# A decode block forward and backward on one core: a regrouped turn between the two passes

## The chip, the cores and the metric

The kernel runs on one core of a Trainium2 chip. The metric is device time in microseconds (us) of one execution, the median of a few runs. The engines are named as in the profile: PE (TensorE; PEld is its weight load), DVE (VectorE), ACT (ScalarE), POOL (GpSimd) and SP (SyncE). In this kernel SP issues nearly all the loads and POOL all the stores; PE, DVE and ACT compute.

## The reference

The reference is a decode step of one token (model width D = 640) and its gradients: adaptive layer norm, attention of 32 heads over a cache of 8192 positions with head width 192, an output projection, then an MLP of width F = 1536 with a second norm inside it. Cut to what matters here:

```
h  = layernorm(x) * (1 + ca) + sa            # sa, ca, ga, sb, cb, gb from silu(c) @ w_mod
q  = h @ wq;  p = softmax(q k^T / sqrt(192));  o = p v;  ao = o @ wo
x  = x + ga * ao
hb = layernorm(x) * (1 + cb) + sb
x1 = hb                                       # the mixer's shift pads a length-1 sequence with zeros
h2 = gelu(layernorm(x1) @ w3) @ w4
out = x + gb * (x1 + h2)
_out, vjp = jax.vjp(f, x, k_cache, v_cache, wq, wo, w3, w4, c, w_mod);  grads = vjp(grad_out)
```

With one token each weight gradient is an outer product: dW4 is 1536x640, the GELU output times the row `dbo` (the incoming gradient times gb). For each head dV is the probability column times the row `do`, and dK is the column dS times the row q; both have the size of the caches, 32 x 8192 x 192. dS needs dP, the sum over the head width of V times `do`, so V is read a second time in the backward pass. `do` comes from `dao` (the gradient at ao) through wo transposed, and `dao` comes through the norms from dn2 = du @ W3 transposed, where du is the gradient at the MLP's hidden layer.

## The kernel before, in words

The cache of one head is handled as two half tiles, t = 0 and 1, of 128 partitions x 32 positions x 192 (1536 KB each). The forward pass runs over heads with a software pipeline (the loop of line 582): step i loads V of head i-1, scales K of head i-1 by the exponentials on ACT and DVE (`fwd_scale`, L394 and L402), and multiplies V and the scaled K on PE (L419, L427, L435). The backward pass goes from head 31 down to 0 (the loop of line 1266): for each head DVE multiplies V by `do` (`bwd_mult`), PE sums it into dP (L1051), DVE and ACT write dV (`bwd_dv`: ACT 20 rows of 32, L1069, and DVE the others, L1036) and DVE writes dK (`bwd_dk`). Weight gradients are jobs put between the heads; `job_dw4` made three blocks of dW4 on ACT per job in steps 17 to 20, and `job_dw3` followed in steps 21 to 25.

Between the passes lies the turn, lines 659 to 1264. It is one chain of small steps:

- W4 and W3 are loaded into three "big" tiles `w_t[0..2]` (`load_wt`, L536 and L539) in the last two forward steps. `dg_some` takes twelve dot products of W4 rows on DVE.
- PE finishes head 31, then the last projection (`last_ao`). In the PE order, the first group of four W3 blocks is transposed between `last_ao(1)` and `last_ao(2)` (`w3T_some`, PE L682 and a copy out of PSUM on ACT or DVE). W3 has 60 blocks; `tr_bank` hands out half a PSUM tile, four blocks, at a time, so the 15 groups alternate over two PSUM tiles of two banks.
- Norm columns, `u_mm` (L747), GELU and its derivative on columns, the rest of the transposes with the `fwd_kvK` of head 31 between them, then dn2 (L812), the second norm's gradient, `dao_bf`, `do` (L934) and its copies `do_pb`.
- The first stores of the kernel's large outputs follow: dV of head 31, first half, is written into `w_t[3]`, the tile that held the transposed W3, and stored in two parts (L1075).

PE, DVE and ACT run in the order in which the code is written (`pin_order`), and SP and POOL issue their DMAs in program order as well: an instruction that waits holds up all behind it on its engine. Buffers come from pools: "big" has five half tiles, used by K tiles, the `w_t` tiles and later by dV and dK; `fv` has three for V, `fpr` two (the forward products, later V), `bv` one, which lies over space that the forward pass frees late. `ring_load` refills V and wo tiles in the backward pass as `bwd_mult` frees them. Loads of V of heads 29 and 30 for the backward pass are issued at the turn: in the code before, V of 29 at line 600 behind W4 and W3, V of 30 in `ring_load` (L330 and L847); V of head 31 stays in its buffers from the forward pass.

Of the kernel before, what the change touches and what calls it, by code (L numbers as in the profile page):

```python
# [20 lines left out]
def kernel(  # L21
# [72 lines left out]
    def bank(tag, bufs=1, name=None, n=512):  # L94
        return psum[0].tile([P, n], FP32, tag=tag, name=name or "ps_" + tag, bufs=bufs)
# [97 lines left out]
    def act_copy(out, in_):  # L193
        nc.scalar.copy(out=out, in_=in_)  # L194
# [130 lines left out]
    def ring_tile(pool):  # L325
        return pool.tile([P, JH, DH], BF16, name="V_sb", tag="prod" if pool is fpr else "V_sb")

    def load_v(pool, h, t):
        tl = ring_tile(pool)
        nc.sync.dma_start(out=tl, in_=V_hd[h][:, t * JH : (t + 1) * JH, :])  # L330
        return tl

    def fwd_load(h, t):
        if 0 <= h < HQ:
            st[h]["V"].append(load_v(fv, h, t))
        if h + 2 < HQ and (h + 2, t) not in K_st:
            K_st[h + 2, t] = load_k(h + 2, t)
# [192 lines left out]
    def alloc_wt(k):  # L530
        w_t.append(flat(big_tile(f"w_t{k}")))
# [50 lines left out]
    for i in range(1, HQ + 1):  # L582
# [7 lines left out]
        if p:  # L590
            fwd_wo(i - 1, st[i - 1])
        if i == HQ - 1:
            alloc_wt(0)
            load_wt(0)
        if i == HQ:
            alloc_wt(1)
            load_wt(1)
            alloc_wt(2)
            load_wt(2)
            V_b[HQ - 3] = [load_v(fpr, HQ - 3, t) for t in range(2)]  # L600
            dg_some(0, 7)
# [65 lines left out]

    tr_n, tr_ps, w3T_next = [0], [None], [0]

    def tr_bank():  # L670
        k = tr_n[0] % 2
        tr_n[0] += 1
        if k == 0:
            tr_ps[0] = bank("s", 2, "t_ps", 1024)
        return tr_ps[0][:, 512 * k : 512 * (k + 1)]

    def w3T_some(n, copy=act_copy):
        for g in range(w3T_next[0], w3T_next[0] + n):
            t_ps = tr_bank()
            for k in range(4):  # L680
                f, i = divmod(4 * g + k, NDC)
                nc.tensor.matmul(t_ps[:, k * P : (k + 1) * P], lhsT=w3n(i, f * P, (f + 1) * P), rhs=ident_bf, start=True, stop=True)  # L682
            copy(w3T(4 * g, 4), t_ps)
        w3T_next[0] += n
# [22 lines left out]
    last_ao(1)  # L707
    w3T_some(1)
    last_ao(2)
# [7 lines left out]
    dot(jk, xs, cb1, s3[:, 2:3])  # L717
    w3T_some(1)
    fwd_keep(LH, sl)
    w3T_some(1)  # L720
    m3 = tn[:, 0:3]
# [10 lines left out]
    nc.vector.tensor_scalar(out=t1, in0=t1, scalar1=v1[:, 0:1], scalar2=None, op0=ALU.add)  # L732
    w3T_some(3)
    hb_bf = ccol(NDC, "hb_bf", BF16)
# [49 lines left out]
    stt(du_bf, deriv, -1.0, d_g, ALU.mult, ALU.mult)  # L784
    w3T_some(4)
    for q in range(2):
        fwd_kvK(LH, q, sl, True)
        w3T_some(1, (act_copy, dve_copy)[q])
    hcb = ccol(NDC, "hcb")
# [7 lines left out]
    mul(nh, n1_c, h1)  # L797
    for q in range(2, 4):
        fwd_kvK(LH, q, sl, True)
        w3T_some(1, (act_copy, dve_copy)[q - 2])  # L800
    w3T_some(1)
    cs = ccol(6, "cs")
# [4 lines left out]
    dot(jk, dbo_c, cb1, cs[:, 4:5])  # L807
    dot(jk, dbo_c, cbn, cs[:, 5:6])
    dn2_ps = bank("b", name="dn2_ps")
    for f in range(NFC):  # L810
        for i in range(NDC):
            nc.tensor.matmul(dn2_ps[:, i : i + 1], lhsT=w3T(f * NDC + i), rhs=du_bf[:, f : f + 1], start=(f == 0 and i == 0), stop=(f == NFC - 1), skip_group_check=True)  # L812
    nc.tensor.matmul(tn[:, 16:22], lhsT=negd_mat, rhs=cs, start=True, stop=True)
    kb_sb = const.tile([P, 2 * DH], FP32, name="kb_sb")
    fek_cm.__exit__(None, None, None)
# [8 lines left out]
    V_b[HS[0]] = st[HS[0]]["V"]  # L824
    held = {("v", HS[2], 0), ("v", HS[2], 1)}
    wo_src = {(PS[k], cc): st[2 * PS[k] + 1]["wo"][:, cc, :] for k in range(2) for cc in range(3)}
# [9 lines left out]
    def ring_load():  # L836
        while ring_n[0] < len(ring) and (ring_n[0] < NR - 2 or ring_key(ring_n[0] - NR) in freed):
            kind, k, t = ring[ring_n[0]]
            pool = (fv, bv, fpr, fpr, fv, fv)[ring_n[0] % NR]
            ring_n[0] += 1  # L840
            if (kind, k, t) in held:
                continue
            if kind == "v":
                V_b.setdefault(k, []).append(load_v(pool, k, t))
                if k == HS[1]:
                    tl = big_tile("V_sb")
                    nc.sync.dma_start(out=tl, in_=V_hd[k][:, JH:J, :])  # L847
                    V_b[k].append(tl)
            else:
                lo, n = PS[BATCHES[k][-1]], len(BATCHES[k])  # L850
                tl = flat(ring_tile(pool))[:, 0 : 3 * n * D].rearrange("p (c r) -> p c r", r=D)
                nc.sync.dma_start(out=tl, in_=wo_v[:, 3 * lo : 3 * (lo + n), :])
                for hp in range(lo, lo + n):
                    for cc in range(3):
                        wo_src[hp, cc] = tl[:, 3 * (hp - lo) + cc, :]
# [28 lines left out]
    def woT_some(n):  # L884
        for j in range(woT_next[0], woT_next[0] + n):
            t_ps = tr_bank()
            for cc in range(3):
                nc.tensor.matmul(t_ps[:, cc * P : (cc + 1) * P], lhsT=sl["wo"][:, cc, j * P : (j + 1) * P], rhs=ident_bf, start=True, stop=True)
            act_copy(woT2[:, j, :], t_ps[:, 0 : 3 * P])
        woT_next[0] += n  # L890

    woT_some(2)
    bwd_pf_act(HS[0])
    bwd_pf_act(HS[1])
    bwd_pf_dve(HS[0])
    bwd_pf_dve(HS[1])
    g_f = ccol(NFC, "g_f")
    mul(g_f, u, sg)
    g_bf = ccol(NFC, "g_bf", BF16)
    dve_copy(g_bf, g_f)  # L900
    s4 = ccol(4, "s4")
# [5 lines left out]
    nc.tensor.matmul(m4, lhsT=negd_mat, rhs=s4, start=True, stop=True)  # L907
    woT_some(3)
    c6 = ccol(6, "c6")
    dve_copy(c6, tn[:, 16:22])  # L910
    td = ccol(NDC, "td")
    zd = ccol(NDC, "zd")
# [11 lines left out]
    m0d = ccol(1, "m0d")  # L924
    dve_copy(m0d, m4[:, 0:1])
    psum_cm.__exit__(None, None, None)
    psum[0] = ctx.enter_context(tc.tile_pool(name="psum_b", bufs=1, space=bass.MemoryType.PSUM, reuse_waits="tile"))
# [3 lines left out]
    do_pb[PS[0]] = bsm.tile([P, 2 * DH], BF16, name="do_pb", tag="do_pb")  # L931
    for c0 in (DH, 0):
        for j in range(NDC):
            nc.tensor.matmul(do_ps[:, c0 : c0 + DH], lhsT=dao_bf[:, j : j + 1].to_broadcast([P, P]), rhs=woT2[:, j, c0 : c0 + DH], start=(j == 0), stop=(j == NDC - 1))  # L934
        act_copy(do_pb[PS[0]][:, c0 : c0 + DH], do_ps[:, c0 : c0 + DH])
    for cc in range(3):
        nc.tensor.matmul(do_ps[:, 400 + cc : 401 + cc], lhsT=do_pb[PS[0]][0:1, cc * P : (cc + 1) * P], rhs=ident_bf[0:1, 0:1], start=True, stop=True)
# [11 lines left out]
    def mid_mm():  # L949
# [4 lines left out]
        mid_ps["kbc"] = kbc_ps  # L954

    def h2_mm():
        for r in range(NDC):
            for f in range(NFC):
                nc.tensor.matmul(h2_ps[:, r : r + 1], lhsT=w4n(f, r * P, (r + 1) * P), rhs=g_bf[:, f : f + 1], start=(f == 0), stop=(f == NFC - 1))

# [162 lines left out]

    def job_dw4(k):
        o = bso.tile([P, 3, D], BF16, name="dw4", tag="so")
        for cc in range(3):
            tsc(o[:, cc, :], dbo_bc, g_f[:, 3 * k + cc : 3 * k + cc + 1], 0)
        st2.dma_start(out=out_7[3 * k * P : 3 * (k + 1) * P, :].rearrange("(c p) r -> p c r", p=P), in_=o)

    def job_dw3(i):  # L1130
# [70 lines left out]
    for k in range(HH):  # L1201
        J1[1 + k].append(lambda hp=PS[k]: job_dwo(hp))
    for k in range(NFC // 3):
        J1[1 + HH + k].append(lambda k=k: job_dw4(k))
    for k in range(NDC):
        J1[1 + HH + NFC // 3 + k].append(lambda i=k: job_dw3(i))

# [42 lines left out]

    h2_mm()
    bwd_dv(HS[0], 0, 0, 2, w_t[3].rearrange("p (j d) -> p j d", d=DH))
    bwd_dv(HS[0], 1)
    dve_copy(do_bf[:, 3 * PS[0] : 3 * PS[0] + 3], do_ps[:, 400:403])
    bwd_dv(HS[1], 0, 8)
    c_first = fin_c(PS[0], 1)
    bcast_dao()
    q_pb[PS[0]] = pair_bc(bsm, q_bf, PS[0], "q_pb")
    act_copy(kb_sb, kb_ps[:, 0 : 2 * DH])
    mid_mm()  # L1260
    bwd_mult(HS[0], 0)
    ring_load()
    bwd_dv(HS[1], 1)
    bwd_mult(HS[0], 1)
    AHEAD = 2 * NPH
    for i in range(HQ):
# [29 lines left out]
        if i in cps:  # L1296
            fin_c_copy(*cps.pop(i))
        if i == 1:
            mid_cols()
            job_mid()  # L1300
            dve_copy(dmod_bf[:, 2 * NDC : 6 * NDC], dmod_c[:, 2 * NDC : 6 * NDC])
# [44 lines left out]
```

## Time and profile before

| | |
|---|---|
| median of 3 runs | 1400.14 us (1400.01 to 1400.24) |
| the profiled execution | 1400.24 us; its span in the trace 1398.4 us |
| PE, DVE, ACT busy | 849.0, 1081.3, 962.2 us |
| moved by DMA | 570.81 MB: 343.08 MB read, 225.91 MB written |
| mean DMA rate over the span | 407 GB/s |
| chain that ended last | DMA 46%, PE 20%, DVE 18%, issue 7%, ACT 6% |

The page cuts the span into 40 slices of 35 us. Digits give the busy share of each engine in tenths, and a row gives the mean share of the 16 DMA engines and what they moved. An answer by windows gives the same for any stretch: busy time and instruction count of PE, PEld, DVE, ACT and POOL, then the granted TensorE clock (PEclk), the DMA share and GB/s. A timeline line gives start and duration, the operation, what it writes and reads, a count where like ones are merged, and in brackets the idle time before it and who ended it. The chain of waits is followed back from the last instruction; it gives start, length and what held the work up. A DMA answer gives the size of a transfer and the time from its issue to its landing.

### The profile page before, as it was taken

The numbers are of one execution on the slowest core, as the hardware profiler recorded it, in microseconds if no ns is written. First come the engines' busy times: TensorE is split into PE (matmuls) and PEld (weight loads), VectorE is DVE, ScalarE is ACT, GpSimd is POOL, SyncE is SP. The second block draws the span as 40 slices with busy tenths as digits, with TensorE's granted clock in tenths as the row PEclk, the third lists the DMA queues.
The fourth block names the chain that finished last, engine by engine and source line by source line (L and its number), as shares of the span: only waits on it lengthen the run. The fifth ranks groups of instructions, "written<-read, shape, count | busy, mean of one in ns | idle before, by whom it ended". The sixth has DMA issues, their size and how long they took to land.

```text
span 1398.4 us, 28097 instructions
## 1 busy us (share of the span) xinstructions
PE 849.0 (61%) x11512; PEld 667.9 (48%) x11512; DVE 1081.3 (77%) x1317; ACT 962.2 (69%) x2622; POOL 111.7 (8%) x203
## 2 busy tenths in 40 slices
PE   3699999999999998546637552334332344324331
PEld 3577777777777776435536441223222232213220
DVE  3678888888888887689988984876677669679794
ACT  1488887787877786683885696467666767558680
POOL 0000000000000000011110111111111111111011
PEclk9799999999999999565656566666676666766665
DMA  9999999999999999588999999999999999999997
GB/s 393 417 420 419 418 419 421 419 421 419 420 409 418 409 406 376 235 345 342 425 428 424 426 429 428 427 429 426 427 426 425 425 422 422 423 413 428 427 429 295
DMA packets 73183, 570.81 MB, mean 408 GB/s; under 512 B 6878, under 2 KB 19934, under 8 KB 32606
## 3 DMA queue, kind: packets, MB, share of 16 engines
q1 hardware_dynamic: 48736, 343.10, 59.5%
q0 software_dynamic: 24288, 225.92, 38.3%
q8 instruction: 90, 1.47, 0.4%
q14 instruction: 39, 0.32, 0.1%
q10 hardware_dynamic: 30, 0.00, 0.0%
HBM read 343.08 MB, written 225.91 MB: 407 GB/s over the span
## 4 chain that ended last, share of the span: by engine, by line
DMA 46%; PE 20%; DVE 18%; issue 7%; ACT 6%; SPq 2%; POOL 0%; another core or an unknown queue 0%; POOLq 0%; DVEq 0%; ACTq 0%
DMA V_sb<-in_A_v_cache_dram 15%; DMA out_dram<-dV 12%; PE ps_a L419 7%; DMA out_dram<-dK 6%; DVE dK L1036 5%; DVE V_sb L131 5%; PE ps_b L427 4%; DMA wq<-in_A_wq_dram 4%; PE S_ps L361 3%; ACT dV L1069 3%; DMA K_sb<-in_A_k_cache_dram 2%; DMA out_dram<-wq_o 2%; DVE dV L1036 2%; DMA out_dram<-dw 2%; PE kb_ps L435 2%
## 5 line engine op out<-in xcount | busy, mean ns | idle before, releaser
L1069 ACT ACTIVATE dV<-do_pb,PF 128x192 bf16<-128x192 bf16 x1248 | 435.5, 440 | 77.6 <-DMA out_dram<-dK 50.8
L1051 PE MATMUL dP_ps<-V_sb,ident_bf 128*128 128x256 bf16 x1536 | 230.0, 325 | 247.0 <-DVE V_sb L131 246.9
L394 ACT ACTIVATE EK<-K_sb,E_f 128x192 bf16<-128x192 bf16 x1024 | 363.6, 441 | 9.4 <-PE kb_ps L299 3.2
L1051 PEld LDWEIGHTS <-ident_bf 128*128 128x128 bf16 x1536 | 178.2, 117 | 298.5 <-issue 176.4
L1036 DVE TENSOR_TENSOR dK<-dS,q_pb 128x6144 bf16<-128x6144 bf16 (+1 forms) x67 | 212.9, 3211 | 39.1 <-DMA out_dram<-dK 35.3
L131 DVE TENSOR_TENSOR prod<-K_sb,q_pb 128x6144 bf16<-128x6144 bf16 x64 | 214.6, 3353 | 35.4 <-DMA K_sb<-in_A_k_cache_dram 34.8
L131 DVE TENSOR_TENSOR V_sb<-V_sb,do_pb 128x6144 bf16<-128x6144 bf16 x64 | 211.9, 3350 | 6.2 <-DMA V_sb<-in_A_v_cache_dram 6.2
L419 PE MATMUL ps_a<-EK,V_sb 128*128 128x193 bf16 x2048 | 199.1, 249 | 23.5 <-DMA V_sb<-in_A_v_cache_dram 22.3
L419 PEld LDWEIGHTS <-V_sb 128*128 128x128 bf16 x2048 | 172.9, 99 | 43.6 <-DMA V_sb<-in_A_v_cache_dram 35.0
L402 DVE TENSOR_TENSOR EK<-K_sb,P2h 128x1536 bf16<-128x1536 bf16 x128 | 121.5, 950 | 0.0
L1036 DVE TENSOR_TENSOR dV<-P2h,do_pb 128x2304 bf16<-128x2304 bf16 (+1 forms) x63 | 84.9, 1374 | 46.4 <-DMA out_dram<-dV 43.8
L427 PE MATMUL ps_b<-EK,V_sb 128*64 128x193 bf16 x2048 | 111.1, 251 | 0.0
L361 PE MATMUL S_ps<-prod,ident_bf 64*64 64x256 bf16 x3072 | 99.8, 277 | 9.3 <-DVE prod L131 8.9
L361 PEld LDWEIGHTS <-ident_bf 64*64 64x64 bf16 x3072 | 83.3, 109 | 24.7 <-issue 24.0
L427 PEld LDWEIGHTS <-V_sb 128*64 128x64 bf16 x2048 | 83.4, 110 | 21.0 <-issue 21.0
L382 ACT ACTIVATE E_f<-sm_ps,negm 128x64 f32<-128x64 f32 x32 | 10.0, 314 | 83.2 <-DVE negm L380 83.2
L435 PE MATMUL kb_ps<-EK,hot_bf 128*32 128x384 bf16 x1024 | 65.9, 335 | 0.0
L1075 POOL DMA_DIRECT2D out_dram<-dV x63 | 33.7, 534 | 399.7 <-ACT dV L1069 248.5
L194 ACT CAST do_pb<-bc_ps 128x384 bf16<-128x384 f32 x15 | 7.0, 470 | 75.9 <-PE bc_ps L190 75.9
L1162 PEld LDWEIGHTS <-ident_bf 128*128 128x128 bf16 x112 | 14.6, 130 | 90.2 <-issue 87.6
L1120 ACT ACTIVATE wq_o<-wq_bc,ha_f 128x1536 bf16<-128x1536 bf16 x12 | 18.5, 1566 | 48.6 <-DMA out_dram<-wq_o 48.6
L1090 POOL DMA_DIRECT2D out_dram<-dK x67 | 37.1, 554 | 183.5 <-DVE dK L1036 146.1
(317 smaller groups left out, 830.1 us busy)
## 6 DMA issues: line engine op xcount, KB each, us to landing
V_sb<-in_A_v_cache_dram SPq DMA_DIRECT2D x126, 1536.0 KB, 16.9
K_sb<-in_A_k_cache_dram SPq DMA_DIRECT2D x64, 1536.0 KB, 18.9
out_dram<-dV POOLq DMA_DIRECT2D x63, 1536.0 KB, 21.4
out_dram<-dK POOLq DMA_DIRECT2D x63, 1536.0 KB, 22.5
wq<-in_A_wq_dram SPq DMA_DIRECT2D x3, 2560.0 KB, 33.8
wo_t<-in_A_wo_dram SPq DMA_DIRECT2D x16, 480.0 KB, 18.1
out_dram<-dwo POOLq DMA_DIRECT2D x16, 480.0 KB, 20.0
wq<-in_A_wq_dram SPq DMA_DIRECT2D x4, 1920.0 KB, 35.9
```

What stands on the lines that cost most here:

```text
L131: nc.vector.tensor_tensor(out=out, in0=a, in1=b, op=ALU.mult)
L361: nc.tensor.matmul(st["S_ps"][c0 : c0 + 64, r, t * JH : (t + 1) * JH, :], lhsT=ident_bf[64 * r : 64 * r + 64, 64 * r : 64 * r + 64], rhs=p ...
L394: nc.scalar.activation(out=EK[:, jj, 0:DH], in_=K_st[h, t][:, r * JQ + jj, :], func=ACT.Copy, scale=st["E_f"][:, j : j + 1])
L402: nc.vector.tensor_tensor(out=EK[:, NA:JQ, 0:DH].rearrange("p j (d r) -> p j d r", r=2), in0=K_st[h, t][:, r * JQ + NA : (r + 1) * JQ, :]. ...
L419: nc.tensor.matmul(st["A_ps"][:, 0 : DH + 1], lhsT=V_sb[:, r * JQ + jj, a0:a1], rhs=EK[:, jj, 0 : DH + 1], start=(q == 0 and jj == 0), sto ...
L427: nc.tensor.matmul(st["B_ps"][g : g + 64, 0 : DH + 1], lhsT=V_sb[:, r * JQ + jj, b0:b1], rhs=EK[:, jj, 0 : DH + 1], start=(q == 0 and jj < ...
L435: nc.tensor.matmul(kb_ps[g : g + 32, 0 : 2 * DH], lhsT=hot_bf[:, HQ - 1 - h : 2 * HQ - 1 - h], rhs=EK[:, jj : jj + 2, 0:DH], start=(h == 0 ...
L1036: nc.vector.tensor_tensor(out=o.rearrange("p j (d r) -> p j d r", r=2), in0=pairs[:, :, None, :].to_broadcast([P, n, NP2, 2]), in1=vec.rea ...
L1051: nc.tensor.matmul(bst[h]["dP_ps"][:, t * JH : (t + 1) * JH, :], lhsT=ident_bf, rhs=V_sb[:, :, k * DS : (k + 1) * DS], start=(k == 0), sto ...
L1069: nc.scalar.activation(out=o[:, jj, :], in_=doh, func=ACT.Copy, scale=bst[h]["PF"][:, j0 + jj : j0 + jj + 1])
L1075: st2.dma_start(out=dV_hd[h][:, j0 + r0 : j0 + r1, :], in_=o[:, r0:r1, :])
L1090: st2.dma_start(out=dK_hd[h][:, j0 : j0 + n, :], in_=o[:, r0 : r0 + n, :])
```

## The change

Four things change, all of them around the turn.

1. `w3T_some(n)` counts blocks instead of groups of four and fills one PSUM tile (up to eight blocks, 1024 columns) before one copy. The 60 blocks go as 4, 8, 8 before `u_mm`, then 8, 8 (this one copied by DVE), 8, 4, 8, 4, the last four with a `fwd_kvK` ahead of each. The columns that DVE computes after `du_bf` stand ahead of these copies. `woT_some` (wo transposed) goes likewise, in groups of two, two and one.
2. V of heads 31 and 30: the forward pass's second half of V of head 30 goes into a big tile; the first half of V of head 31 is loaded one step earlier, ahead of W4's first nine rows; V of 29 (both halves) is loaded ahead of the rest of W4 and the first part of W3, V of 30 (first half) ahead of W3's second part, and its second half behind it. The old loads in `ring_load` go.
3. dW4 is made at the turn: `dw4_some` multiplies `dbo_bc` by a column of the GELU output on DVE, twelve times, into the parts of `w_t[2]` and `w_t[1]` where W3 was, and POOL stores it in three transfers of 6, 3 and 3 blocks. `job_dw4` goes, and `job_dw3` moves to steps 17 to 21.
4. The order at the start of the backward pass: `h2_mm` now stands between the two halves of `do`; the copies of dao and q (`bcast_dao`, `pair_bc`), the probabilities of head 30 (`bwd_pf`) and `bwd_mult(31, 0)` come ahead of dV of head 30, and `mid_mm` moves behind dK of head 31.

```
     def fwd_load(h, t):
-        if 0 <= h < HQ:
-            st[h]["V"].append(load_v(fv, h, t))
+        if 0 <= h < HQ and len(st[h]["V"]) == t:
+            st[h]["V"].append(load_v(big if (h, t) == (HQ - 2, 1) else fv, h, t))
...
         if i == HQ - 1:
+            fwd_load(HQ - 1, 0)
             alloc_wt(0)
             load_wt(0)
         if i == HQ:
+            V_b[HQ - 3] = [load_v(fpr, HQ - 3, t) for t in range(2)]
             alloc_wt(1)
             load_wt(1)
+            V_b[HQ - 2] = [load_v(fv, HQ - 2, 0)]
             alloc_wt(2)
             load_wt(2)
-            V_b[HQ - 3] = [load_v(fpr, HQ - 3, t) for t in range(2)]
+            V_b[HQ - 2].append(load_v(big, HQ - 2, 1))
             dg_some(0, 7)
...
     def w3T_some(n, copy=act_copy):
-        for g in range(w3T_next[0], w3T_next[0] + n):
-            t_ps = tr_bank()
-            for k in range(4):
-                f, i = divmod(4 * g + k, NDC)
-                nc.tensor.matmul(t_ps[:, k * P : (k + 1) * P], lhsT=w3n(i, f * P, (f + 1) * P), rhs=ident_bf, start=True, stop=True)
-            copy(w3T(4 * g, 4), t_ps)
+        b0 = w3T_next[0]
+        t_ps = bank("s", 2, "t_ps", 1024)[:, 0 : n * P]
+        for k in range(n):
+            f, i = divmod(b0 + k, NDC)
+            nc.tensor.matmul(t_ps[:, k * P : (k + 1) * P], lhsT=w3n(i, f * P, (f + 1) * P), rhs=ident_bf, start=True, stop=True)
+        copy(w3T(b0, n), t_ps)
...
     last_ao(0)
     last_ao(1)
-    w3T_some(1)
+    w3T_some(4)
     last_ao(2)
...
+    w3T_some(8)
+    w3T_some(8, dve_copy)
+    for q, n in enumerate((8, 4, 8, 4)):
+        fwd_kvK(LH, q, sl, True)
+        w3T_some(n)
     dn2_ps = bank("b", name="dn2_ps")
...
+    W4_O = (6, 3, 3)
+
+    def dw4_some(n):
+        for f in range(dw4_n[0], dw4_n[0] + n):
+            tl, c0 = (w_t[2], f * D) if f < W4_O[0] else (w_t[1], W4_R * D + (f - W4_O[0]) * D)
+            nc.vector.tensor_scalar(out=tl[:, c0 : c0 + D], in0=dbo_bc, scalar1=g_f[:, f : f + 1], scalar2=None, op0=ALU.mult)
+            if f + 1 in (W4_O[0], W4_O[0] + W4_O[1], NFC):
...
-    woT_some(2)
-    bwd_pf_act(HS[0])
-    bwd_pf_act(HS[1])
-    bwd_pf_dve(HS[0])
-    bwd_pf_dve(HS[1])
-    g_f = ccol(NFC, "g_f")
-    mul(g_f, u, sg)
-    g_bf = ccol(NFC, "g_bf", BF16)
-    dve_copy(g_bf, g_f)
+    bwd_pf_act(HS[0])
+    woT_some(2)
+    dw4_some(2)
     s4 = ccol(4, "s4")
...
     dve_copy(c6, tn[:, 16:22])
+    dw4_some(1)
...
     dve_copy(m0d, m4[:, 0:1])
+    bwd_pf_dve(HS[0])
+    dw4_some(4)
...
+    do_half(DH)
+    for r in range(NDC):
+        for f in range(NFC):
+            nc.tensor.matmul(h2_ps[:, r : r + 1], lhsT=w4n(f, r * P, (r + 1) * P), rhs=g_bf[:, f : f + 1], start=(f == 0), stop=(f == NFC - 1))
+    do_half(0)
...
-    h2_mm()
     bwd_dv(HS[0], 0, 0, 2, w_t[3].rearrange("p (j d) -> p j d", d=DH))
+    dw4_some(5)
     bwd_dv(HS[0], 1)
-    dve_copy(do_bf[:, 3 * PS[0] : 3 * PS[0] + 3], do_ps[:, 400:403])
-    bwd_dv(HS[1], 0, 8)
-    c_first = fin_c(PS[0], 1)
     bcast_dao()
     q_pb[PS[0]] = pair_bc(bsm, q_bf, PS[0], "q_pb")
-    act_copy(kb_sb, kb_ps[:, 0 : 2 * DH])
-    mid_mm()
+    bwd_pf(HS[1])
     bwd_mult(HS[0], 0)
     ring_load()
+    bwd_dv(HS[1], 0, 8)
+    dve_copy(do_bf[:, 3 * PS[0] : 3 * PS[0] + 3], do_ps[:, 400:403])
+    bwd_mult(HS[0], 1)
+    c_first = fin_c(PS[0], 1)
     bwd_dv(HS[1], 1)
-    bwd_mult(HS[0], 1)
+    act_copy(kb_sb, kb_ps[:, 0 : 2 * DH])
```

More of the change, by code (lines that the diff above doesn't have):

```diff
@@ L325, in ring_tile @@
     def ring_tile(pool):
-        return pool.tile([P, JH, DH], BF16, name="V_sb", tag="prod" if pool is fpr else "V_sb")
+        return pool.tile([P, JH, DH], BF16, name="V_sb", tag="prod" if pool is fpr else "big" if pool is big else "V_sb")
     def load_v(pool, h, t):
@@ L666, in w3T @@
         return w_t[2][:, c0 : c0 + n * P]
[L668 to L675, printed above, removed]
-    def w3T_some(n, copy=act_copy):
-        for g in range(w3T_next[0], w3T_next[0] + n):
-            t_ps = tr_bank()
-            for k in range(4):
-                f, i = divmod(4 * g + k, NDC)
-                nc.tensor.matmul(t_ps[:, k * P : (k + 1) * P], lhsT=w3n(i, f * P, (f + 1) * P), rhs=ident_bf, start=True, stop=True)
-            copy(w3T(4 * g, 4), t_ps)
+    w3T_next = [0]
+    def w3T_some(n, copy=act_copy):
+        b0 = w3T_next[0]
[4 more added lines that the diff above has]
+        copy(w3T(b0, n), t_ps)
         w3T_next[0] += n
@@ L717 @@
     dot(jk, xs, cb1, s3[:, 2:3])
-    w3T_some(1)
+    w3T_some(8)
     fwd_keep(LH, sl)
-    w3T_some(1)
     m3 = tn[:, 0:3]
@@ L732 @@
     nc.vector.tensor_scalar(out=t1, in0=t1, scalar1=v1[:, 0:1], scalar2=None, op0=ALU.add)
-    w3T_some(3)
+    w3T_some(8)
     hb_bf = ccol(NDC, "hb_bf", BF16)
@@ L784 @@
     stt(du_bf, deriv, -1.0, d_g, ALU.mult, ALU.mult)
[L785 to L788, printed above, removed]
     hcb = ccol(NDC, "hcb")
@@ L797 @@
     mul(nh, n1_c, h1)
[L798 to L801, printed above, removed]
     cs = ccol(6, "cs")
@@ L808 @@
     dot(jk, dbo_c, cbn, cs[:, 5:6])
+    g_f = ccol(NFC, "g_f")
+    mul(g_f, u, sg)
+    g_bf = ccol(NFC, "g_bf", BF16)
+    dve_copy(g_bf, g_f)
+    w3T_some(8)
+    w3T_some(8, dve_copy)
+    for q, n in enumerate((8, 4, 8, 4)):
+        fwd_kvK(LH, q, sl, True)
+        w3T_some(n)
     dn2_ps = bank("b", name="dn2_ps")
@@ L813 @@
     nc.tensor.matmul(tn[:, 16:22], lhsT=negd_mat, rhs=cs, start=True, stop=True)
+    dw4_n = [0]
+    W4_O = (6, 3, 3)
[4 more added lines that the diff above has]
+            if f + 1 in (W4_O[0], W4_O[0] + W4_O[1], NFC):
+                m = W4_O[0] if f < W4_O[0] else W4_O[1]
+                nc.gpsimd.dma_start(out=out_7[(f + 1 - m) * P : (f + 1) * P, :].rearrange("(c p) r -> p c r", p=P), in_=tl[:, c0 - (m - 1) * D : c0 + D].rearrange("p (c r) -> p c r", r=D))
+        dw4_n[0] += n
     kb_sb = const.tile([P, 2 * DH], FP32, name="kb_sb")
@@ L824 @@
     V_b[HS[0]] = st[HS[0]]["V"]
-    held = {("v", HS[2], 0), ("v", HS[2], 1)}
+    held = {("v", HS[1], 0), ("v", HS[2], 0), ("v", HS[2], 1)}
     wo_src = {(PS[k], cc): st[2 * PS[k] + 1]["wo"][:, cc, :] for k in range(2) for cc in range(3)}
@@ L844, in ring_load @@
                 V_b.setdefault(k, []).append(load_v(pool, k, t))
[L845 to L848, printed above, removed]
             else:
@@ L884, in woT_some @@
     def woT_some(n):
[L885 to L889, printed above, removed]
+        j0 = woT_next[0]
+        t_ps = bank("s", 2, "t_ps", 1024)[:, 0 : 3 * n * P]
+        for k in range(3 * n):
+            j, cc = j0 + k // 3, k % 3
+            nc.tensor.matmul(t_ps[:, k * P : (k + 1) * P], lhsT=sl["wo"][:, cc, j * P : (j + 1) * P], rhs=ident_bf, start=True, stop=True)
+        act_copy(woT2[:, j0 : j0 + n, :].rearrange("p j m -> p (j m)"), t_ps)
         woT_next[0] += n
+    bwd_pf_act(HS[0])
     woT_some(2)
-    bwd_pf_act(HS[0])
-    bwd_pf_act(HS[1])
-    bwd_pf_dve(HS[0])
-    bwd_pf_dve(HS[1])
-    g_f = ccol(NFC, "g_f")
-    mul(g_f, u, sg)
-    g_bf = ccol(NFC, "g_bf", BF16)
-    dve_copy(g_bf, g_f)
+    dw4_some(2)
     s4 = ccol(4, "s4")
@@ L907 @@
     nc.tensor.matmul(m4, lhsT=negd_mat, rhs=s4, start=True, stop=True)
-    woT_some(3)
+    woT_some(2)
+    woT_some(1)
     c6 = ccol(6, "c6")
     dve_copy(c6, tn[:, 16:22])
+    dw4_some(1)
     td = ccol(NDC, "td")
@@ L931, with do_half @@
     do_pb[PS[0]] = bsm.tile([P, 2 * DH], BF16, name="do_pb", tag="do_pb")
-    for c0 in (DH, 0):
+    def do_half(c0):
         for j in range(NDC):
@@ L954, in mid_mm @@
         mid_ps["kbc"] = kbc_ps
[L956 to L959, printed above, removed]
     def mid_cols():
@@ L1122, in tsc @@
             nc.vector.tensor_scalar(out=out, in0=in_, scalar1=col, scalar2=None, op0=ALU.mult)
[L1124 to L1128, printed above, removed]
     def job_dw3(i):
@@ L1202 @@
         J1[1 + k].append(lambda hp=PS[k]: job_dwo(hp))
-    for k in range(NFC // 3):
-        J1[1 + HH + k].append(lambda k=k: job_dw4(k))
     for k in range(NDC):
-        J1[1 + HH + NFC // 3 + k].append(lambda i=k: job_dw3(i))
+        J1[1 + HH + k].append(lambda i=k: job_dw3(i))
     def add_outer(at, name, view, lo, n, col_bf, rows_f, dram, acc, first):
@@ L1297 @@
             fin_c_copy(*cps.pop(i))
+        if i == 0:
+            mid_mm()
         if i == 1:
```

## The prediction

> **What bounds the kernel now.** I read the page's slices first, then windows around the dip in the middle, then the DMA issues there, the chain of waits and the timelines.
>
> ```profile
> DMA  9999999999999999588999999999999999999997
> GB/s 393 417 420 419 418 419 421 419 421 419 420 409 418 409 406 376 235 345 342 425 428 424 426 429 428 427 429 426 427 426 425 425 422 422 423 413 428 427 429 295
> ```
>
> The transfers run full except in slices 15 to 18, the turn. The windows say where:
>
> ```profile
> 558.00:568.00 10.00, 6.82 (x110) 5.13 (x109) 4.24 (x27) 6.38 (x14) 0.00 (x0) 0.54 0.78 327
> 568.00:576.00 8.00, 5.40 (x114) 3.88 (x107) 3.84 (x29) 2.84 (x7) 0.00 (x0) 0.93 0.56 182
> 576.00:600.00 24.00, 14.04 (x133) 10.79 (x131) 20.23 (x34) 20.15 (x57) 2.68 (x5) 0.50 0.48 199
> 640.00:646.00 6.00, 6.00 (x38) 4.59 (x37) 5.96 (x5) 0.00 (x0) 0.54 (x1) 0.65 0.26 64
> 700.00:1380.00 680.00, 275.71 (x1721) 207.26 (x1721) 525.15 (x402) 455.21 (x1182) 95.00 (x168) 0.66 1.01 425
> ```
>
> Idle DMA time is (1 - share) x length: 2.2 + 3.5 + 12.5 + 4.4 = 22.6 us. After 646 the share is 1.0 to the end: no engine's speed matters there, only bytes. So the change is worth what it does to the idle time of the turn. That turn is a chain of small steps, and it starts when W3 has landed:
>
> ```profile
> w_t<-in_B_w_dram SPq DMA_DIRECT2D x1, 1152.0 KB, 14.1
> w_t<-in_B_w_dram SPq DMA_DIRECT2D x1, 768.0 KB, 12.1
> w_t<-in_B_w_dram SPq DMA_DIRECT2D x1, 480.0 KB, 10.7
> ...
> 538.97 3.36 SPq L539 DMA_DIRECT2D w_t<-in_B_w_dram  x1
> 542.38 1.20 SPq L330 DMA_DIRECT2D V_sb<-in_A_v_cache_dram  x1
> ```
>
> W3's second part (`w_t[2]`) is issued at 538.97 and lands at 553.1; V of 29, behind it, is issued at 542.38 and lands at 556.7 (14.3 in its own answer). The chain and the timelines:
>
> ```profile
> 521.02 16.78 DMA w_t<-in_B_w_dram
> ...
> 554.97 0.26 PE t_ps L682 x4
> ...
> 571.11 1.48 PE dn_ps L812 x60
> ...
> 594.96 7.75 PE dP_ps L1051 x48
> ```
>
> ```profile
> 555.05 0.27 PE L704 MATMUL turn_ps<-o_col_bf,wo_t 128*128 128x1 bf16 x5
> 578.89 3.43 DVE L1036 TENSOR_TENSOR w_t<-P2h,do_pb 128x3072 bf16<-128x3072 bf16 x2 [1.36 <-ACT do_pb L194]
> 603.90 3.36 DVE L1036 TENSOR_TENSOR dK<-dS,q_pb 128x6144 bf16<-128x6144 bf16 x1
> ```
>
> PE reaches the first transposes at 554.83, 1.7 us after W3 is there, and does not wait. The last V half, issued at 546.61, has no landing record; one half tile after V of 30's first (545.09 + 19.0 = 564.1) makes 567.8. So before, 14.7 us of V loads cover the chain behind W3.
>
> **Loads.** Transfers land in the order of issue, one V half every 3.6 to 3.8 us (530.3, 533.9, then `w_t[0]` 537.8 by the chain, 541.6 for V of 31, from issue plus time to landing), also where the mean share falls: some DMA engines trail and stay busy, and a transfer has landed when its last part has. Filling the small gaps at 520 to 536 therefore brings no landing forward. What counts is what stands ahead. Ahead of `w_t[0]` there is now one more V half: 537.8 + 3.7 = 541.5. Ahead of `w_t[2]` there are three more (29 twice, 30 once): 553.0 + 3 x 3.65 = 564.0. The last load still ends at 567.7. SP's waits don't undo this: the K tiles whose places the loads take are scaled by 540 (ACT's rows L394, 2.8 us a quarter), well ahead of these landings.
>
> The late `w_t[0]` delays `dg_some` on DVE, behind it the head's sum, PE's matmuls of head 31 and `last_ao(0)`: 3.7 us, to about 558.8. The group of four transposes in front of `last_ao(2)` then needs `w_t[2]`, and PE takes its work in order: `last_ao(2)` moves from 555.05 to 564.1, **+9.1**. The first delay vanishes in the second.
>
> **Transposes.** A copy of 384 columns takes 0.48 us on ACT, of 512 0.58, so of 1024 about 0.98; on DVE 512 take 0.69, 1024 about 1.25. Before, `u_mm` started 0.8 us after its column was ready, held by a transpose waiting for its copy; with two full tiles in flight it doesn't: **-0.8**. From `du_bf` (564.6) to the end of dn2 (572.6) before took 7.9 us. After: two groups of eight and a `fwd_kvK` (1.0, 1.0, 0.8 us at half clock), the DVE copy, which starts only when the moved columns and g_f are done (1.9 us after du) and so ends at +3.2, then groups and `fwd_kvK` 0.5 + 0.8 + 1.0 + 0.8 + 0.5 and dn2's 60 matmuls, 1.64 to 2.2: 8.4 at half clock, 7.2 at full. **+0.1**, ends -0.7 and +0.5.
>
> **From dn2 to dV.** Before, the reductions of dn2 started 2.25 us late, behind `P2h` and g_f, which waited for ACT's PF (DVE idle 1.80 in front of `P2h`); these go, the m4 matmul comes 0.95 us after dn2 instead of 2.97: **-2.0**. dW4's instructions: 128x1536 takes 0.614 us on DVE (L1122), 128x1280 0.546, so 128x640 about 0.38. Two lie in DVE's wait for dn2, one lies in the chain (+0.4), four run while PE and ACT make `do_pb` and overrun it by 0.35. **+0.75**. First dV: 9.1 - 0.8 + 0.1 - 2.0 + 0.75 = +7.1.
>
> **From do_pb to dK.** Before, 578.86 to 603.90: 25.0 us. After, ACT's second `do_pb` copy stands behind `h2_mm` (1.76) and comes 2.6 us after the first; then twenty dV rows (7.0, as in L1069's x20), the copies of dao and q and PF (1.7): 11.3. DVE, done with its own dV by then (it idles some 5 us for PF, where before it had dV of head 30 to do), takes `P2h` 0.25, V 3.35, dV of 30 2.55, V 3.35, sums 0.75, dV 1.35, three wo rows 2.45, their sums 0.9, dP 0.7, dS 0.35: 27.3 in all, **+2.3**. The gain of taking `mid_mm`'s 2.5 us out of PE's way is in it: PE no longer ends last. SP waits longer too: V of 28 is loaded when dP of head 31 is done, 604.7 instead of 600.1, with nothing late by it.
>
> First dK: 7.1 + 2.3 = +9.4. From there DVE does the same work at 21 us a head up to where DMA ran empty (640 to 645), so the point at which transfers become the bound comes 9.4 later.
>
> **dW4's bytes.** 1.97 MB leave that bound phase. Its stores, at 25.9 to 26.5 GB/s on each of 16 engines (425 GB/s in the windows), take 4.7 us; they now run in the gap behind the turn, which has room (12 us idle by my sum ahead of them). **-4.7**. POOL issues three (0.76 each by L1128's row) where it is idle. ACT loses twelve rows of 0.81 us in a phase bound by DMA: nothing; if that cover were gone, up to 9.7 us would be saved there, but share 1.01 excludes that. dW3 four steps earlier: the same bytes, nothing.
>
> **Sum.** +9.4 - 4.7 = +4.7. Counted the other way, by gaps: loads end at 567.7, wo's batch starts behind the last `fwd_kvK` at 580 (12.3 idle, before 4.5), then 2.6 to the first dW4 store, 1.1 and 4.1 between dV stores, before 5.9, 2.1, 4.5 and 0.5: 20.1 against 17.5, and at the second gap 5.8 against 5.0: +3.4. I take +4 between them: span 1402.4, time 1404.2 from the profiled execution's 1400.24, which is the highest of the three runs and 0.1 above the median.
>
> The granted clock enters here: 0.54 in 558 to 568, 0.93 behind it, 0.50 from 576. The Trainium skill, "TensorE: Matmul & The Clock Gate", section "What's actually happening", says that about 3.4 us of idle PE put it back to half clock and as much busy time frees it. By that page the 5 us for which PE would now wait for W3 cost half clock afterwards, and the sum would be +4.7; by a clock that is full up to dn2 it would be about +2.7. The trace's drop to 0.50 in a stretch where PE waits agrees.
>
> **Rivals.**
> - *W3 does not gate.* Its wait vanishes if `w_t[2]` lands by 558.8, so 5 us earlier than I say; for it speaks that the DMA share dips at 520 to 536 and loads are now issued earlier, against it the landings in strict step. Only `w_t[0]`'s 3.7 remains: 4.0 - 5.4 = -1.4, 1398.8.
> - *Nothing is late (other side).* If the trailing engines catch up in the filled gaps, both land as before: 4.0 - 9.1 = -5.1, 1395.1. It decides from a landing of `w_t[2]` before about 557.
> - *The new order costs more.* If DVE's wait for head 30's PF, or dV of 30 standing behind dW4's store in its buffer, also pushes ACT's next forty rows past DVE, some 5 us come on top: 1409.
> - *The head of the backward pass gains.* If DVE's stall is hidden by a DMA that is full there, +2.3 becomes nothing or less: 1401.5.
>
> **Numbers.** Forecast 0.60; W3 not gating 0.10; nothing late 0.12; order costs more 0.10; hidden stall 0.08. The likeliest own range is 1401.5 to 1407; for 8 in 10 I go to 1397.5 and 1409. A run of this kernel tells about 0.2% (2.8 us) from no change: faster 0.13, same 0.23 (not gating, hidden stall, and the forecast's low end), slower 0.64.
>
> **What would show it.** Right: V of 29 issued near 530, `w_t[2]` landing near 564, PE idle some 5 us in front of the third transpose, the first store (dW4) near 587, DVE idle about 5 us ahead of `bwd_mult(31, 0)`, full share from about 655. Wrong: `w_t[2]` landing before 559, or a first dV store before 585.

## The result

The changed kernel takes 1402.36 us (median of 11 runs, 1401.19 to 1403.64) against 1399.49 us before (11 runs): a ratio of 1.0025, 95% interval 1.0015 to 1.0034. It is slower by 2.9 us; the forecast was slower by 4, 1404.2. The profiled execution took 1402.17 us, its span 1400.4 us, 2.0 more than the profiled span before.

The slices of the page in GB/s (the row of DMA digits is the same as before):

```profile
GB/s 393 418 420 418 418 420 419 420 420 420 419 408 420 411 417 381 193 340 337 425 427 424 428 426 428 427 428 427 426 427 425 425 425 418 426 418 423 429 429 303
```

The same hole at the turn, with slice 16 at 193 GB/s where it had 235. The windows of the changed kernel, in the columns explained above:

```profile
562.00:580.00 18.00, 13.56 (x226) 10.44 (x227) 8.88 (x59) 9.53 (x16) 0.00 (x0) 0.62 0.18 64
580.00:602.00 22.00, 9.39 (x115) 7.07 (x113) 16.77 (x33) 18.16 (x51) 5.19 (x7) 0.57 0.78 293
602.00:646.00 44.00, 15.50 (x108) 12.30 (x106) 41.35 (x70) 34.33 (x97) 5.05 (x9) 0.66 0.99 388
646.00:653.00 7.00, 5.71 (x35) 4.28 (x35) 6.97 (x5) 2.13 (x3) 0.39 (x1) 0.62 0.24 99
653.00:1380.00 727.00, 315.77 (x1966) 241.56 (x1963) 578.87 (x479) 481.50 (x1263) 99.06 (x177) 0.66 1.01 424
```

Idle DMA time, (1 - share) x length, is 14.8 + 4.8 + 0.4 + 5.3 = 25.3 us from 562 to 653. The kernel before, over the same stretch, has 9.7 and 8.8 in the first two windows and 5.1 behind them (share 0.90 in both of those), 23.6 in all; the 22.6 of the prediction left out some shorter stretches and does not compare. The first two lines of the kernel before:

```profile
562.00:580.00 18.00, 12.14 (x168) 8.01 (x164) 8.75 (x55) 8.20 (x19) 0.00 (x0) 0.69 0.46 170
580.00:602.00 22.00, 13.21 (x133) 10.78 (x134) 17.67 (x24) 18.39 (x53) 2.82 (x5) 0.55 0.60 242
```

The difference, 1.7 us from shares of two digits, agrees with the loss that the spans show, 2.0: the bytes are the same 570.81 MB and from 653 on the share is full in both. The hole has moved: now most of it lies ahead of 580, between the last load and the first work that the turn hands on.

Why the turn hands on late, from the DMA answers (size and time to landing), SP's timeline, PE's waits and PE's timeline:

```profile
525.01 0.38 SPq L536 DMA_DIRECT2D w_t<-in_B_w_dram  x1
w_t<-in_B_w_dram SPq DMA_DIRECT2D x1, 1440.0 KB, 16.5
...
543.14 0.38 SPq L539 DMA_DIRECT2D w_t<-in_B_w_dram  x1
w_t<-in_B_w_dram SPq DMA_DIRECT2D x1, 1152.0 KB, 20.8
```

```profile
PE t_ps L678 <- DMA w_t<-in_B_w_dram: 4.6, 1, 4.6
...
563.99 0.40 PE L678 MATMUL t_ps<-ident_bf,w_t 128*128 128x128 bf16 x2 [4.61 <-DMA w_t<-in_B_w_dram]
564.17 0.32 PE L700 MATMUL turn_ps<-o_col_bf,wo_t 128*128 128x1 bf16 x5
```

W4's first nine rows land at 541.5 and W3's second part at 563.9, 10.9 us later than before. PE, done with head 31, waits 4.6 us for it, and `last_ao(2)` starts at 564.17 instead of 555.05. On DVE:

```profile
583.90 3.42 DVE L1041 TENSOR_TENSOR w_t<-P2h,do_pb 128x3072 bf16<-128x3072 bf16 x2
...
594.72 0.23 DVE L879 CAST P2h<-PF 128x128 bf16<-128x128 f32 x1 [4.65 <-ACT PF L875]
594.86 3.35 DVE L131 TENSOR_TENSOR V_sb<-V_sb,do_pb 128x6144 bf16<-128x6144 bf16 x1
...
611.41 3.36 DVE L1041 TENSOR_TENSOR dK<-dS,q_pb 128x6144 bf16<-128x6144 bf16 x1
```

The first dV comes 5.0 us later than before (578.89), the first dK 7.5 (603.90), with a wait of 4.65 us for ACT in between. Of these 7.5 us, dW4's stores, taken out of the bound stretch, give back about 5 (e5, below).

### The profile page after: what moved, and what is told of

Same layout as the page of the kernel before. It is cut to its first block, busy times and chain, and to the rows that moved or that the text cites. A ratio compares the mean times of both kernels' runs of the same rounds, so it can differ in the third digit from the quotient of the medians.

```text
span 1400.4 us, 28087 instructions
## 1 busy us (share of the span) xinstructions
PE 851.4 (61%) x11512; PEld 670.5 (48%) x11512; DVE 1084.7 (77%) x1328; ACT 952.1 (68%) x2603; POOL 111.3 (8%) x202
## 2 busy tenths in 40 slices
DMA packets 73168, 570.81 MB, mean 408 GB/s; under 512 B 6863, under 2 KB 19919, under 8 KB 32591
## 5 line engine op out<-in xcount | busy, mean ns | idle before, releaser
L361 PEld LDWEIGHTS <-ident_bf 64*64 64x64 bf16 x3072 | 84.2, 110 | 24.7 <-issue 24.1
```

The source lines that it names most:

```text
L361: nc.tensor.matmul(st["S_ps"][c0 : c0 + 64, r, t * JH : (t + 1) * JH, :], lhsT=ident_bf[64 * r : 64 * r + 64, 64 * r : 64 * r + 64], rhs=p ...
```

## The experiments

The kernel before was timed anew beside each group of runs (medians 1398.18 to 1399.49 us), so the runs are compared best by their ratio to it; the changed kernel stands at 1.0025.

**Loads as before, all else as changed (e1).** The edit, and the moved lines put back:

```
-            V_b[HQ - 3] = [load_v(fpr, HQ - 3, t) for t in range(2)]
             alloc_wt(1)
             load_wt(1)
-            V_b[HQ - 2] = [load_v(fv, HQ - 2, 0)]
             alloc_wt(2)
             load_wt(2)
-            V_b[HQ - 2].append(load_v(big, HQ - 2, 1))
+            V_b[HQ - 3] = [load_v(fpr, HQ - 3, t) for t in range(2)]
```

> The changed kernel with the loads of V of heads 29, 30 and 31 as before the change; the rest as changed. My theory (W3 lands late behind three V halves and holds the turn): W3's second part lands at 553 instead of 564, PE does not wait for it, the first dV store comes 8.9 us earlier and so does the end: some 9 us under the changed kernel, about 1393. Rival (the loads' order is hidden, the new order of the rest costs the time): within 2 us of the changed kernel, 1402.

Measured: 1392.14 us, ratio 0.9953 (0.9939 to 0.9967), 10.2 us under the changed kernel by the medians. PE's timeline of this run has no wait at the transposes:

```profile
554.76 0.39 PE L697 MATMUL turn_ps<-o_col_bf,wo_t 128*128 128x1 bf16 x10
555.01 0.38 PE L675 MATMUL t_ps<-ident_bf,w_t 128*128 128x128 bf16 x4
555.23 0.27 PE L697 MATMUL turn_ps<-o_col_bf,wo_t 128*128 128x1 bf16 x5
```

W3 lands at 553.0, the first dV starts at 574.41 and the first dK at 602.17. The order and places of these loads alone turn the change from a gain of 7 us into a loss of 3.

**The new loads alone, in the kernel before (e2).** The same lines in the other direction.

> The kernel before with the new order and places of the V loads alone. My theory: PE waits about 5 us for W3, which lands at 564, and the whole turn comes 9.1 us later with nothing to make up for it: about 1408. Rival (loads issued earlier fill gaps and the other parts cost the time): 1399.5 or less.

Measured: 1409.08 us, ratio 1.0078 (1.0065 to 1.0090). PE waits 4.1 us for W3, which lands at 564.0; the first dK starts at 613.26, 9.4 later than before. So the loss doesn't need the rest of the change, and in the kernel before nothing makes up for it.

**W4 and W3 ahead of V of 29 and 30, V of 31's first half still ahead of W4 (e3).**

```
+            alloc_wt(1)
+            load_wt(1)
+            alloc_wt(2)
+            load_wt(2)
             V_b[HQ - 3] = [load_v(fpr, HQ - 3, t) for t in range(2)]
-            alloc_wt(1)
-            load_wt(1)
-            V_b[HQ - 2] = [load_v(fv, HQ - 2, 0)]
-            alloc_wt(2)
-            load_wt(2)
-            V_b[HQ - 2].append(load_v(big, HQ - 2, 1))
+            V_b[HQ - 2] = [load_v(fv, HQ - 2, 0)]
+            V_b[HQ - 2].append(load_v(big, HQ - 2, 1))
```

> The changed kernel with V of 29 and 30 loaded behind all of W4 and W3, but V of 31's first half still ahead of W4's first nine rows. My theory: W3 lands at 553 as before, W4's rows still at 541.5, 3.7 us late, so the dot products of W4 and with them PE are 3.7 us late and PE comes to the first transposes at 558.9 without waiting: 5 us under the changed kernel, about 1397.4. Rival (only W3's landing counts): the same time as with all loads as before, about 1393.

Measured: 1397.29 us, ratio 0.9987 (0.9978 to 0.9996). W3 lands at 552.9, W4's rows at 541.7, and PE comes to `last_ao(2)` without a wait for W3. It is late by the dot products: DVE's last scaled keys of head 31 come 3.7 us later than in e1 (549.49 against 545.75), PE's first `last_ao` 4.5 later (559.24 against 554.76):

```profile
559.49 0.38 PE L678 MATMUL t_ps<-ident_bf,w_t 128*128 128x128 bf16 x4
559.71 0.27 PE L700 MATMUL turn_ps<-o_col_bf,wo_t 128*128 128x1 bf16 x5
```

The half tile ahead of W4 costs about 5 us by itself (e3 against e1), and the three ahead of W3 another 5 (the changed kernel against e3): both delays are there, and in the changed kernel the second hides the first.

**Probabilities of head 30 made at the turn (e4).**

```
     bwd_pf_act(HS[0])
+    bwd_pf_act(HS[1])
...
     bwd_pf_dve(HS[0])
+    bwd_pf_dve(HS[1])
...
-    bwd_pf(HS[1])
     bwd_mult(HS[0], 0)
```

> The changed kernel with one step moved: the probabilities of head 30 (PF on ACT, P2h on DVE) are made at the turn beside those of head 31, so that the V product of head 31 does not wait for ACT's twenty dV rows. My theory: DVE's idle time of 4.65 us ahead of it goes, the first dK comes 4.4 us earlier, and so the end: about 1398. Rival (DMA is full there, or PE or ACT takes the wait's place): 1401 to 1402.

Measured: 1397.74 us, ratio 0.9989 (0.9980 to 0.9998), 4.6 us under the changed kernel. DVE goes straight on:

```profile
588.19 1.35 DVE L1043 TENSOR_TENSOR dV<-P2h,do_pb 128x2304 bf16<-128x2304 bf16 x1
589.46 3.35 DVE L131 TENSOR_TENSOR V_sb<-V_sb,do_pb 128x6144 bf16<-128x6144 bf16 x1
...
606.12 3.36 DVE L1043 TENSOR_TENSOR dK<-dS,q_pb 128x6144 bf16<-128x6144 bf16 x1
```

From the first dV to the first dK it takes 22.8 us, against 27.5 in the changed kernel and 25.0 before: the new order is better than the old one once its one wait is gone (e6 below has the old order beside the same probabilities).

**dW4 by the jobs, as before (e5).** `dw4_some` and its calls taken out, `job_dw4` and its place in the list put back.

> The changed kernel with dW4 made by the jobs between heads 15 to 12 as before, on ACT, and not at the turn. My theory: the turn's chain gets some 0.6 us shorter (three or four instructions of 0.38 us), and 1.97 MB of stores go back into the stretch that DMA bounds, 4.7 us: about 4 us over the changed kernel, 1406.5. Rival (these stores are hidden wherever they are): 0.6 us under it, 1401.8.

Measured: 1406.73 us, ratio 1.0063 (1.0051 to 1.0076), 4.4 us over the changed kernel by the medians and 5.3 by the ratios. dW4 at the turn is worth its bytes: the stores fill idle time, and the first dK is at 611.27 without it and 611.41 with it, so that its instructions cost nothing that lasts.

**The start of the backward pass in the old order (e6).** The last block of the diff undone (with `mid_mm` put back ahead of `bwd_mult(31, 0)`), the probabilities of head 30 at the turn.

> The changed kernel with the start of the backward pass in the old order (dV of head 30's first half ahead of the copies of dao and q, the key sums on PE ahead of dP of head 31, probabilities of head 30 made at the turn). My theory: DVE's idle time for these probabilities goes, but PE's 2.5 us of key sums stand ahead of dP again and dW4's five instructions stay on DVE: from do_pb to the first dK 26 to 27 us instead of 27.5, 1 us under the changed kernel, 1401.4. Rival (the order is the whole cost of that stretch): 2.7 us under it or more, 1399.7.

Measured: 1399.72 us, ratio 1.0010 (1.0001 to 1.0019), 2.6 us under the changed kernel. My figure was 1; the rival's 2.7 is what came. From the first dV to the first dK it took 24.7 us (583.95 to 608.61), about as long as before the change (25.0): dP on PE ends last there, DVE waits 3.0 us for it, and dW4's five instructions, 1.6 us, fit into that wait. Against e4, which differs in the order alone, the old order takes 1.9 us longer in this stretch.

**Four blocks to a copy (e7).** Two groups share a tile, as before:

```
     def w3T_some(n, copy=act_copy):
-        t_ps = bank("s", 2, "t_ps", 1024)[:, 0 : n * P]
-        for k in range(n):
+        t_ps = bank("s", 2, "t_ps", 1024)
+        for g in range(n // 4):
+            half = t_ps[:, 512 * g : 512 * g + 512]
...
+            copy(w3T(b0, 4), half)
```

> The changed kernel with each copy of transposed W3 taking four blocks, as before, in the new order of the work around them. My theory: eight blocks a copy are worth little by themselves, 0.5 us of the chain: 1402.9, not to be told from the changed kernel. Rival (they made all of the 2.4 us that the chain gained between the norm's column and dn2): 1404.8.

Measured: 1409.54 us, ratio 1.0079 (1.0065 to 1.0093): 7 us over the changed kernel, three times what even the rival expected. From the end of `u_mm` to the end of dn2 it took 14.6 us instead of 8.7. PE's timeline:

```profile
573.41 1.01 PE L680 MATMUL t_ps<-ident_bf,w_t 128*128 128x128 bf16 x8 [1.37 <-ACT w_t L194]
576.29 0.59 PE L680 MATMUL t_ps<-ident_bf,w_t 128*128 128x128 bf16 x4 [1.87 <-DVE w_t L197]
...
578.85 0.58 PE L680 MATMUL t_ps<-ident_bf,w_t 128*128 128x128 bf16 x4 [0.67 <-ACT w_t L194]
...
582.71 0.59 PE L680 MATMUL t_ps<-ident_bf,w_t 128*128 128x128 bf16 x4 [0.67 <-ACT w_t L194]
```

In this run PE starts a second group of a tile only when the copy of the first has ended, and stops for the DVE copy too. The granted clock differs as well: it was 0.50 from 564 to 608 here, where the changed kernel had its full clock from 576.3 to 583.1. How much of the 7 us that is, no run separates from the waits. In the changed kernel the same stretch has two short waits:

```profile
573.41 1.03 PE L678 MATMUL t_ps<-ident_bf,w_t 128*128 128x128 bf16 x8
575.54 0.59 PE L678 MATMUL t_ps<-ident_bf,w_t 128*128 128x128 bf16 x4 [0.34 <-ACT w_t L194]
576.80 0.61 PE L678 MATMUL t_ps<-ident_bf,w_t 128*128 128x128 bf16 x8 [0.15 <-ACT w_t L194]
```

**Four blocks, each group in a tile of its own (e9),** to tell the shared tile from the number of copies:

```
-        t_ps = bank("s", 2, "t_ps", 1024)
         for g in range(n // 4):
             b0 = w3T_next[0]
-            half = t_ps[:, 512 * g : 512 * g + 512]
+            t_ps = bank("s", 2, "t_ps", 1024)[:, 0 : 4 * P]
```

> The changed kernel with four blocks a copy again, but each group of four takes a PSUM tile of its own (half of it unused), so that PE need not wait for the copy of the other half of the same tile. Theory (in the run with four blocks and two groups to a tile, PE waits at each second group for the copy just started, 1.28 us a group): those waits go, some stay because the two groups copied by DVE hold both tiles until DVE's columns are done; from the end of u_mm to the end of dn2 about 12 us instead of 14.6 (8.7 in the changed kernel): 1405.5. Rival (the number of copies costs, each with its fixed part): 1409, as with four blocks in shared tiles.

Measured: 1405.83 us, ratio 1.0046 (1.0032 to 1.0060). So about half of e7's loss comes with the shared tile. Waits for ACT of 0.94 us and for DVE of 1.05 remain, and dn2 ends 9.0 us after the start of du (573.01 to 582.01), against 12.4 in e7 and 6.5 in the changed kernel. The clock is a rival here too: it was full from 579.8, 3.5 us later than in the changed kernel.

**The transposes alone, in the kernel before (e10).** `w3T_some` and its calls as in the diff, the rest untouched.

> The kernel before with the transposes of the changed one alone (up to eight blocks a copy, the columns ahead of them; wo's transposes as before). My theory: u_mm starts 0.7 us earlier, dn2 ends some 1.8 us sooner behind du, and all behind it moves by that: 2.5 us under the kernel before, about 1396.5. Rival (DVE waits for head 31's probabilities behind ACT's copies of wo anyway): no change.

Measured: 1395.95 us, ratio 0.9975 (0.9965 to 0.9985), 3.3 us under the kernel before. `u_mm` and du start 0.7 sooner, dn2 ends 2.8 sooner (569.80) and dK starts 2.4 sooner (601.50). Here as well the full clock came sooner, at 566.3 instead of 569.1, and is in these 2.8 us.

**Both remedies (e8): the loads as before and the probabilities of head 30 at the turn.**

> The changed kernel with the loads as before and the probabilities of head 30 made at the turn. My theory: both gains add up, 8.9 and 4.4 us, since the one ends ahead of do_pb and the other begins behind it: about 1389, under both kernels. Rival (DMA is full early, so the second gain has no idle time to take): 1393, as with the loads alone.

Measured: 1386.03 us, ratio 0.9913 (0.9900 to 0.9927): 12 us under the kernel before and 16 under the changed one, the fastest of all. The gains add up: 10.2 in e1 and 4.6 in e4 make 14.8. The windows of this run:

```profile
562.00:580.00 18.00, 12.61 (x220) 9.34 (x219) 14.47 (x61) 11.05 (x25) 3.60 (x5) 0.69 0.69 251
632.00:640.00 8.00, 7.29 (x48) 5.50 (x47) 7.97 (x10) 1.27 (x2) 1.49 (x3) 0.72 0.51 170
640.00:1380.00 740.00, 314.40 (x1950) 240.21 (x1950) 576.73 (x474) 481.66 (x1263) 98.52 (x176) 0.66 1.00 422
```

The share in 562 to 580 is 0.69, where the changed kernel has 0.18. What is left idle there is 5.6 us, and 3.9 around 636, where DVE is full.

## Why the prediction was right, step by step

- *Loads land in the order of issue, and filling the dips brings no landing forward.* Right: `w_t[0]` 541.5 (said 541.5), `w_t[2]` 563.9 (564.0), and the loads end as before: the DMA share falls to 0.15 before and 0.10 after in 566 to 568, and to 0.00 behind it. e1, e2 and e3 show that this step carries the sign. The rivals "W3 does not gate" and "nothing is late" fell.
- *`last_ao(2)` +9.1.* Right: 564.17 against 555.05.
- *Transposes.* The term of the sum that was most off. To the start of `u_mm` I had a gain of 0.8; it was 0.4 (+8.7 there), since the 1024-column copy, 1.01 us, stands ahead of the copies that the norm waits for, and the column itself came 9.5 late. From the end of du to the end of dn2 I had 7.9 + 0.1, with ends -0.7 and +0.5: it took 6.3 us (573.36 to 579.66), so -1.6, outside those ends. The step that failed is "the DVE copy, which starts only when the moved columns and g_f are done (1.9 us after du) and so ends at +3.2, then groups": the copy ended at 576.17, 2.8 after du, but PE's next group started at 575.54, 2.2 after du, right behind the ACT copy that had ended at 575.49, and did not wait for DVE. My sum has every group behind the DVE copy wait for it. That is 1.0 of the 1.7 us by which I missed; the other 0.7 lies in the groups and dn2, for which I had taken a value between half and full clock and which ran almost wholly at full clock, granted from 576.3 on.
- *From dn2 to dV, -2.0 + 0.75.* It was 4.2 us against 6.3, so -2.1, 0.8 more of a gain than I said. The reductions came 0.03 us after dn2 (-2.2). dW4's instructions cost about what I said: the one in the chain 0.3, and dV started 0.3 behind `do_pb` for the four. What the sum lacks is the clock at `do`. Its first five matmuls took 0.60 us instead of 0.99, since the clock was full up to 583.1, where before it was 0.50 from 575.9 on. Before and after:

```profile
577.51 0.99 PE L934 MATMUL do_ps<-woT,dao_bf 128*128 128x192 bf16 x5
...
582.66 0.60 PE L938 MATMUL do_ps<-woT,dao_bf 128*128 128x192 bf16 x5 [1.21 <-DVE m0d L197]
```

  First dV: +5.0 instead of +7.1.
- *From do_pb to dK, +2.3.* Right: 27.5 us from dV against 25.0, so +2.5, with the wait for PF (4.65, said some 5). That this wait is the cost is shown by e4.
- *dW4's bytes, -4.7.* Right within the intervals: e5 gives 4.4 to 5.3.
- *Sum.* dK +7.5 (said +9.4), less about 5: 2.0 by the spans, 2.9 by the medians (said 4). The count of gaps gave +3.4 and was nearer than the chain's +4.7; over 562 to 653 the windows give 1.7. By the counts above, about 1 of the 2 us by which dV came sooner than forecast is the clock, whose return at 576.3 the sum did not have; so far the nearness of the figure hangs on luck, and the sign does not.
- *Signs.* Most came as said. V of 29 was issued at 534.7 (said near 530), the first store of dW4 at 584.0 (said near 587), and the first dV store at 585.97, 1 us from the bound of 585 that would have spoken against me.

The rivals of "the new order costs more" and "the stall is hidden" fell as well: nothing came on top, and the stall's 4.65 us are worth 4.6 us of the end (e4), so no full DMA hid it. The measured time alone would not have decided that: 1402.4 lies nearer to the hidden stall's 1401.5 than to my 1404.2.

The page of the Trainium skill that I weighed, "TensorE: Matmul & The Clock Gate", section "What's actually happening", agrees with this wait: PE was idle from 559.4 on, its granted clock dropped to 0.50 at 562.6, 3.2 us later, and it stayed there up to 576. It agrees less with the drop of the kernel before, which I had counted for it: there the clock fell at 575.9, and PE's longest pause ahead of that was 2.4 us (573.2 to 575.6). The half clock did not bring the time to the 4.7 that I had worked out for it, since PE did not wait for the DVE copy and the clock was full again ahead of the last groups, dn2 and `do`. My other figure, +2.7 with a clock full up to dn2, lies near the 2.9 measured, but its condition did not hold: the clock was at half for most of the transposes.

## What to carry to other kernels

In this kernel the loads landed in the order of issue, and the spacing of the landings, 3.6 to 3.8 us for a half tile, told what one more transfer ahead costs. So look there first at the end of a phase that runs on loads: place first what starts a chain, and let bulk that nobody awaits yet cover the chain. A dip in the mean share of the DMA engines was no proof of room: before the change it fell to 0.56 in 530 to 532 while the landings kept their step, and the moved loads ended no sooner. A step moved ahead on one in-order engine takes its inputs with it: DVE's 4.65 us of waiting came from one small cast whose input stood behind twenty rows on ACT, and moving that input too turned a loss into a small gain (ratio 1.0025 to 0.9989).

## What the runs showed of the hardware that was not expected

After the wait for W3, PE worked almost without a break from 568.8 on and had its full granted clock again only at 576.3, 7.5 us later; in the run with the loads as before it took from 559.4 to 565.0, 5.7 us. Both are longer than the about 3.4 us of busy time that the Trainium skill names on that page, "TensorE: Matmul & The Clock Gate", section "What's actually happening". And a copy of 1024 columns out of PSUM took 0.99 to 1.01 us on ACT and 1.22 on DVE where one of 512 took 0.58 and 0.69, so that two halves take longer than the whole; on top of that PE stood still for 0.67 to 1.87 us ahead of the groups of e7 that are shown.
